# A one-core attention-and-MLP gradient kernel: the key feature gradient computed in its transposed layout

## The chip, the cores and the metric

The kernel runs on one core of a Trainium2 chip. The metric is the device time of one execution in microseconds (us). Three timed runs of the kernel before gave a median of 820.01 us.

## What is computed

One pre-norm layer is run forward and differentiated: 2048 rows (S) of 640 features (D), a linear-attention block with 32 heads of 20 features, and a gated MLP of width 1728 (F). The outputs are the layer's result and the gradients of the input, of `wqkv`, `wo`, `w1`, `w3` and `w2`. Cut to what matters:

```python
h  = x + A(layernorm(x));   h2 = h + B(layernorm(h))          # forward

def A(x, wqkv, wo):                       # linear attention
    q, k, v = split_heads(x @ wqkv)
    phi = lambda t: where(t > 0, t + 1, exp(t)) + 1e-6
    pq, pk = phi(q), phi(k)
    kv, z = pk^T v, sum_s(pk)             # per head
    o = (pq kv) / (pq . z + 1e-6)
    return o @ wo

def B(x, w1, w3, w2):                     # gated MLP
    return (silu(x @ w1) * (x @ w3)) @ w2

grads = vjp(h2 wrt x, wqkv, wo, w1, w3, w2)(grad_out)
```

The change is about the gradient of k, the input of `phi`. Since phi'(k) = min(pk, 1) up to the small constant, that gradient is `g_k = (xn @ gm + gz) * min(pk, 1)`, where `xn` is the normalised input, `gm` a 640x640 matrix (value weights times the gradient of `kv`) and `gz` the gradient of z, one number for each of the 640 features.

## The kernel before

The schedule is written by hand: every engine runs its instructions in the order of the code, and each DMA queue (SP's, ACT's and POOL's) does too. P = 128, the rows are 16 tiles of 128 (ST), the features five blocks of 128 (DT), W = 512 is a chunk of four row tiles, HD = 320. `dma` and `dmaT` are plain and transposing DMAs issued by SP, `dmaG` plain ones issued by POOL. The stages, with their times in the profile:

- 0 to about 84 us: layer norm, q and k, the key sums. `r_row(t)` makes row tile t of the normalised query features (`pqs[t]`), `r_T(t)` turns it into `pqT` by an SP transpose, `r_head` does both, and `r_store` writes it to DRAM (`r_d`) from POOL's queue.
- about 85 to 340 us: attention output, second layer norm (`f2_hn`, `f2_ht`), MLP forward. The row buffers of tag `pql` are four; `f2_hn(2)` takes the one that held `pqs[4]`.
- 340 to 535 us: gradients of w2 and of the MLP's input and attention's output. They end with `g_q` (the gradient of q, 16 row tiles) and `q_parts` (20 pieces of the gradient of kv), during which SP turns pieces into `QT` and loads turned weights and inputs (`load_xnT`, `load_wqT`).
- 560 to 611 us, called stage D here: small squares (`square`, `unload`), then the loop over 16 row tiles that makes `g_k`: ten matmuls of 320 columns with `xnT` as weights, a VectorE add of `gzb` (gz laid out as a row on all partitions, made by five matmuls with `ones`), and a VectorE op that takes min(pk, 1) and multiplies. `pk` comes in as eight row loads (`load_pk`). `fill(n)` puts n half jobs of the query weight gradient (eight matmuls of 320 columns each) between them; a job's result goes through `obs`, which has ten slots of 320 columns, and out by POOL's queue. Five squares for the value weight gradient are put in at t = 2, 5, 8, 11, 14; they too go out through `obs`, square n into slot pair k = 4, 0, 1, 2, 3.
- 611 to 698 us, stage E: `e_T(t, k)` turns row tile t of `g_q` and of `g_k` by SP transposes; `e_gxn(t)` multiplies 15 turned blocks (5 of q, 5 of k, 5 of `pkT`) with `wqT` and finishes the input's gradient (`ln_bwd`); jobs of the key weight gradient (`wq_jobs((1,))`) fill in before t = 0 and at every third t.
- 698 to 815 us, stage F: the w1 and w3 gradients, from `hnN` (rows of the second layer norm) and blocks `gb` that SP loads turned, 496 rows at a time, into two buffers.

PSUM tiles: `d_acc` takes two banks and has three buffers in stage D (tag `dkv`); it serves the g_k products, the squares and the small transposes in turn.

Of the kernel before, what the change touches and what calls it, by code (L numbers as in the profile page):

```python
# [9 lines left out]
P = 128  # L10
BF16 = mybir.dt.bfloat16
F32 = mybir.dt.float32
# [43 lines left out]
def kernel(  # L56
# [48 lines left out]
    def pool(name, side="left", space=None):  # L105
        kw = dict(space=space) if space is not None else dict(side=side)
        return tc.alloc_tile_pool(name=name, bufs=1, reuse_waits="tile", **kw)
# [195 lines left out]
    def phi_rest(keep=0):  # L303
        while len(held) > keep:
            held.pop(0)()
# [53 lines left out]
    def r_prod(t):  # L359
        for j in range(2):  # L360
            js = slice(j * HD, (j + 1) * HD)
            if t < 8:
                pr[t, j] = (p1.tile([P, HD], F32, name="pr", bufs=2) if t % 2 else
                            pf.tile([P, HD], F32, name="pr", tag="h2", bufs=2))[:]
            else:
                pr[t, j] = ps.tile([P, 512], F32, name="prp", tag="at", bufs=2)[:, 0:HD]
            (G if t < 8 else V).tensor_tensor(out=pr[t, j], in0=pqs[t][:, js], in1=Zb[:, js], op=ALU.mult)
# [16 lines left out]
    def r_T(t):  # L384
        dmaT(out=pqT[:, :, t * P:(t + 1) * P], in_=pqs[t])
# [47 lines left out]
    def m_end(m, js=(0, 1)):  # L433
        mb = mbs[:, m % 4, :]
        acc = macc[m]
        for j in js:
            A.copy(out=mb[:, j * HD:(j + 1) * HD], in_=acc[j][:, 0:HD])
        if m < 2:
            A.copy(out=Z[:, m:m + 1], in_=acc[1][:, HD:HD + 1])
            z_diag(m)  # L440
        if m < DT - 1:
            dmaT(out=mT[:, :, m * P:(m + 1) * P], in_=mb)
# [139 lines left out]
    def r_head(t):  # L582
        r_row(t)
        r_T(t)
# [24 lines left out]
    phi_rest()  # L609
    m_part(3, range(5))  # L610
    q_tile(6)
    r_head(1)
    r_prod(3)
    phi_rest()
    m_part(3, range(5, 11))
# [4 lines left out]
    phi_rest()  # L620
    m_part(3, range(11, ST))
    m_end(3)
    r_T(2)
    load_w2T(4 * P, 8 * P)
    dmaG(out=m_v[:, 1:4, :], in_=mbs[:, 1:4, :])
# [4 lines left out]
    kvT_block(1, big())  # L630
    r_row(4)
    r_prod(6)
    phi_rest()
    m_part(4, range(5, 11))
    q_tile(9)
# [308 lines left out]
    def kv3():  # L944
# [5 lines left out]
        (f2_wT, 4), (phi_rest,), (q_late, 14), (r_T, 4), (r_head, 5), (load_x, 4, 6), (r_prod, 7),  # L950
        (q_out, 10, 14), (mlp_ghh, 4),
        (q_late, 15), (w2_room,), (sig_table,), (f2_half, 0, 0), (f2_half, 1, 0), (f2_half, 2, 0), (f2_half, 3, 0), (mlp_ghh, 5),
        (f2_half, 0, 1), (r_store, 4, 5), (f2_half, 1, 1), (f2_hn, 0), (r_store, 5, 6), (f2_half, 2, 1), (f2_hn, 1),
        (f2_half, 3, 1), (f2_m_out,),
        (f2_half, 4, 0, True), (mlp_ghh, 6), (f2_half, 4, 1, True), (f2_half, 5, 0, True), (r_red, 6, (0,)), (f2_hn, 2), (f2_hn, 3),
        (f2_ht, 2), (f2_ht, 3), (load_w2T, 8 * P, 10 * P), (mlp_ghh, 7), (r_red, 6, (1,)), (r_inv, 6), (r_scale, 6),
        (r_T, 6), (f2_rest,), (r_red, 7), (r_inv, 7), (r_scale, 7), (r_T, 7), (r_store, 6, 7))
# [279 lines left out]
    def load_xnT(c):  # L1237

        if c % 2 == 0:
            both = ba.tile([P, 2, DT, W], BF16, name="xnT", tag="ggb", bufs=2)  # L1240
            xnT[c], xnT[c + 1] = both[:, 0], both[:, 1]
        dmaT(out=xnT[c], in_=xn_d[c * W:(c + 1) * W, :])
# [55 lines left out]
    def load_wqT(k):  # L1298
        dmaT(out=wqT[:, k * DT:(k + 1) * DT, :], in_=A_wqkv[:, k * D:(k + 1) * D])
# [11 lines left out]
    part(3)  # L1311
    load_xnT(1)
    part(4)
    part(4)
    part(20)
    load_xnT(2)
    V.reduce_sum(out=gz[:], in_=gz8[:], axis=AX.X)


# [72 lines left out]
        if i > 1:  # L1392
            fill(1)
    br.release()
    bo.release()
    bv = pool("bv")
    pkT = bv.tile([P, DT, S], BF16, name="pkT")
    small = bv.tile([P, ST, D], BF16, name="small", tag="hnN")
    mN, gkv_b, gm = (small[:, n:n + DT] for n in (0, DT, 2 * DT))
    gzd = small[:, 3 * DT, :].rearrange("p (m q) -> p m q", q=P)  # L1400
    dx = pool("dx", "right")

    def load_pk(c):
        pkb[c] = dx.tile([P, 2, D], BF16, name="pkb", bufs=4)
        (dma if c < 4 else dmaG)(out=pkb[c][:], in_=pk_v[:, c * 2:(c + 1) * 2, :])

    gzb = dx.tile([P, D], F32, name="gzb")
    g_k = gqkv[1] = U1.tile([P, ST, D], BF16, name="g_k", tag="S0")
    load_pk(0)
    load_pk(1)  # L1410
    dma(out=mN, in_=m_v)
    dma(out=rows(dwoT_d), in_=dwoT[:])
    load_pk(2)
    load_pk(3)
    load_xnT(3)
    load_wqT(0)

    for i, (c, ms) in enumerate(SQ_BLOCKS):
        unload(square(wqT[:, 2 * DT:, :], gkvT, i), gm[:, i, :])
        tr = ps.tile([P, len(ms), P], BF16, name="trk", tag="dkv", bufs=3)  # L1420
        for k, m in enumerate(ms):
            T.transpose(tr[:, k, :], gkvT[:, m, c * P:(c + 1) * P], ident[:])
        V.tensor_copy(out=gkv_b[:, c, ms[0] * P:(ms[-1] + 1) * P].rearrange("p (i q) -> p i q", q=P), in_=tr[:])
        fill(1)
        if i == 0:
            for m in range(DT):
                V.tensor_scalar(out=gzd[:, m, :], in0=ident[:], scalar1=gz[:, m:m + 1], scalar2=None, op0=ALU.mult)
        dmaT(out=wqT[:, 2 * DT:, i * P:(i + 1) * P], in_=gm[:, i, :])
    acc = d_acc()
    for m in range(DT):  # L1430
        T.matmul(acc[:, m // 4, m % 4 * P:(m % 4 + 1) * P], lhsT=ones[:], rhs=gzd[:, m, :], start=(m % 4 == 0),
                 stop=True, skip_group_check=True)
    for x, y, bank in ((0, 4 * P, 0), (4 * P, D, 1)):
        A.copy(out=gzb[:, x:y], in_=acc[:, bank, 0:y - x])

    for t in range(ST):
        c, i = divmod(t, TPC)
        u = t // 2
        acc = d_acc()
        for j in range(2):  # L1440
            for k in range(DT):
                T.matmul(acc[:, j, 0:HD], lhsT=xnT[c][:, k, i * P:(i + 1) * P], rhs=gm[:, k, j * HD:(j + 1) * HD],  # L1442
                         start=(k == 0), stop=(k == DT - 1))
        gp = dx.tile([P, D], F32, name="gp")
        V.tensor_tensor(out=two(gp[:]), in0=acc[:, :, 0:HD], in1=two(gzb[:]), op=ALU.add)
        V.scalar_tensor_tensor(out=g_k[:, t, :], in0=pkb[u][:, t % 2, :], scalar=1.0, in1=gp[:], op0=ALU.min,
                               op1=ALU.mult)
        if t % 2 and t < 13:
            fill(1)

        if t in (2, 5, 8, 11, 14):
            n = t // 3
            acc = square(mN, gkv_b, n)
            k = (4, 0, 1, 2, 3)[n]
            ob = obs[:, k * D:(k + 1) * D]
            unload(acc, ob)
            dmaG(out=out2S[:, n, 2 * D:3 * D], in_=ob)
        if t % 2 and u + 4 < 8:
            load_pk(u + 4)
        if t == 2:  # L1460
            load_wqT(1)
        if t in (6, 8, 10, 12):
            n = t // 2 - 3
            dmaT(out=pkT[:, :, n * W:(n + 1) * W], in_=pk_d[n * W:(n + 1) * W, :])
    for _ in jobs:
        pass
    dx.release()
# [1 line left out]


    ex = pool("ex", "right")
    hnN = bv.tile([P, ST, D], BF16, name="hnN")
    blocks = [(f0, min(f0 + NB, 2 * F)) for f0 in range(0, 2 * F, NB)]
    NB0 = 160

# [13 lines left out]
    def load_hnN(i):  # L1489
        dma(out=hnN[:, i * TPC:(i + 1) * TPC, :], in_=hn_v[:, i * TPC:(i + 1) * TPC, :])  # L1490

    gT = {}

    def e_T(t, k):
        if k == 0:
            gT[t] = (ex.tile([P, 2 * DT, P], BF16, name="gT") if t % 3 == 2 else
                     bd[:, 2 * (t % 3):2 * (t % 3) + 2, :].rearrange("p c (k q) -> p (c k) q", q=P))
        dmaT(out=gT[t][:, k * DT:(k + 1) * DT, :], in_=gqkv[k][:, t, :])

    def e_gxn(t):  # L1500
        acc = ps.tile([P, 2, 512], F32, name="gxn", tag="gxn", bufs=2)
        for j in range(2):
            for k in range(15):
                g = gT[t][:, k, :] if k < 2 * DT else pkT[:, k - 2 * DT, t * P:(t + 1) * P]
                T.matmul(acc[:, j, 0:HD], lhsT=g, rhs=wqT[:, k, j * HD:(j + 1) * HD], start=(k == 0),  # L1505
                         stop=(k == 14))
        gx = scr[:, t % 2, :]
        ln_bwd(acc, t, xnN[:, t, :], ln1, gx, g_h[:, t, :], ex, scr[:, 2 + t % 2, :], scr[:, 4, :])()
        return gx
# [3 lines left out]
    njob = 2  # L1513
    jobs = wq_jobs((1,))
    scr = U1.tile([P, DT, D], BF16, name="scr", tag="W6")
    for t in range(3):
        for k in range(2):
            fill(2)
            e_T(t, k)
    for t in range(ST):  # L1520
        if t > 1 and t % 3 == 0:
            fill(2)
        gx = e_gxn(t)
        if t + 3 < ST:
            for k in range(2):
                e_T(t + 3, k)
        dma(out=out1S[:, t, :], in_=gx)
        if t in (2, 3, 5, 6):
            load_hnN((2, 3, 5, 6).index(t))
        if t in (7, 9, 12):  # L1530
            load_block(0, (t - 7) // 2 * NB0, (t - 5) // 2 * NB0 if t < 12 else NB)
        if t == 13:
            load_block(1)
    for _ in jobs:
        pass

# [32 lines left out]
            gw2_turn(i)  # L1569
    ps.release()  # L1570
    ex.release()
    bv.release()
    bl.release()
    U1.release()
# [31 lines left out]
```

## Time and profile before

| | |
|---|---|
| median of three runs | 820.01 us (819.78 to 821.04) |
| profiled execution | 819.99 us |
| its span, first to last instruction | 817.9 us |
| TensorE matmul busy | 811.8 us, 5261 instructions |
| VectorE, ScalarE, GpSimd busy | 452.7, 324.8, 131.8 us |
| mean granted TensorE clock | 1.000 |
| DMA moved | 162.46 MB |

A view's line names the source line, the engine, the operation, what it writes and reads, and the shape. In a timeline the first number is the start in us from the span's start, the second the time to the end of the group, and "x10" the number of instructions that were merged. Matmuls are pipelined, so the spacing of starts, not the duration, says what one costs. About 2.1 us of the execution lie outside the span.

### The profile page before, as it was taken

To read this page: it belongs to the slowest core of one execution; us is meant where nothing else is said; L and a number is where in the kernel's file an instruction comes from. 1 tells how busy PE (TensorE), PEld (TensorE's weight loads), DVE (VectorE), ACT (ScalarE), POOL (GpSimd) and SP (SyncE) were. 2 spreads that over 40 slices of the span, in tenths; PEclk is the share of its full clock that TensorE was granted. 3 is DMA by queue.
4 is the path that set the end of the run, shared out by engine and by line. 5 is a ranking of instruction groups with operands and counts; after the bars stand their busy time and mean duration, and the time that the engine had idled before them with its cause. 6 is when DMAs were issued, how large, how long until landed. Compare 5 with 4: busy or idle time off the path is not lost.

```text
span 817.9 us, 13715 instructions
## 1 busy us (share of the span) xinstructions
PE 811.8 (99%) x5261; PEld 501.6 (61%) x5292; DVE 452.7 (55%) x973; ACT 324.8 (40%) x609; POOL 131.8 (16%) x198
## 2 busy tenths in 40 slices
PE   9999999999999999999999999999999999999998
PEld 6777544555555555754577777777777777544444
DVE  7859997998898566300057777772781544200000
ACT  7856688665565666011222212222212334211111
POOL 2243333333222212100001111110220000000000
PEclk9999999999999999999999999999999999999999
DMA  9799899696485556999967877266997888979991
GB/s 268 201 243 287 198 270 319 196 242 174 126 211 157 165 175 168 230 238 243 260 176 182 214 198 196 58 113 142 252 206 158 182 193 158 240 179 233 218 242 37
DMA packets 335761, 162.46 MB, mean 199 GB/s; under 512 B 252304, under 2 KB 328944, under 8 KB 335696
## 3 DMA queue, kind: packets, MB, share of 16 engines
q1 hardware_dynamic: 291936, 120.68, 63.9%
q0 software_dynamic: 7328, 24.48, 9.2%
q10 hardware_dynamic: 36432, 16.42, 8.0%
q8 instruction: 41, 0.67, 0.4%
q14 instruction: 24, 0.20, 0.1%
HBM read 47.09 MB, written 53.43 MB: 123 GB/s over the span
## 4 chain that ended last, share of the span: by engine, by line
PE 98%; ACT 1%; DVE 1%; issue 0%; POOL 0%; ACTq 0%
PE mm L395 20%; PE job L1335 20%; PE ghn L1131 14%; PE gxn L1505 8%; PE gw L1086 7%; PE big L268 4%; PE o L913 4%; PE o L859 3%; PE gwo L1219 3%; PE macc L430 3%; PE gr L1188 3%; PE dkv L1442 3%; PE at L657 2%; PE mm L268 1%; PE dkv L1369 1%; PE gp L395 1%
## 5 line engine op out<-in xcount | busy, mean ns | idle before, releaser
L1335 PE MATMUL job<-gb,hnN 128*128 128x496 bf16 (+3 forms) x576 | 116.8, 366 | 0.0
L1131 PEld LDWEIGHTS <-ggb 128*128 128x128 bf16 x864 | 84.5, 98 | 33.0
L395 PE MATMUL mm<-pqT,w 128*128 128x512 bf16 x396 | 93.2, 379 | 0.5
L1335 PEld LDWEIGHTS <-hnN 128*128 128x128 bf16 x576 | 55.7, 98 | 61.1
L395 PEld LDWEIGHTS <-w 128*128 128x128 bf16 x540 | 52.5, 98 | 63.2 <-issue 0.6
L1339 ACT CAST obs<-job 128x496 bf16<-128x496 f32 (+4 forms) x56 | 28.5, 509 | 123.7 <-PE job L1335 123.7
L1131 PE MATMUL ghn<-w13a,ggb 128*128 128x320 bf16 x448 | 63.5, 299 | 0.0
L1146 DVE SCALAR_TENSOR_TENSOR wb<-gs,hnb 128x640 f32<-128x640 bf16 x16 | 13.2, 825 | 88.1 <-ACT gs L1143 88.1
L1131 PE MATMUL ghn<-w13b,ggb 128*128 128x320 bf16 x416 | 61.4, 299 | 0.0
L395 PE MATMUL mm<-g2T,w2T 128*128 128x512 bf16 x228 | 58.9, 379 | 0.6
L1086 PE MATMUL gw<-hb,g 128*128 128x512 bf16 (+2 forms) x316 | 58.4, 345 | 0.2
L1086 PEld LDWEIGHTS <-g 128*128 128x128 bf16 x320 | 31.3, 98 | 27.0
L420 ACT CAST ghh<-mm 128x512 bf16<-128x512 f32 x48 | 28.1, 585 | 47.6 <-PE mm L395 41.2
L1196 POOL TENSOR_TENSOR sz<-Zb,g_h 128x640 f32<-128x640 bf16 x16 | 20.2, 1261 | 163.8 <-DVE g_h L1197 163.8
L796 ACT ACTIVATE sig<-mm 128x512 bf16<-128x512 f32 x56 | 33.7, 602 | 25.5 <-PE mm L395 21.7
L1143 ACT ACTIVATE gs<-ghn 128x640 bf16<-128x640 f32 x16 | 11.2, 703 | 75.9 <-PE ghn L1131 66.1
L395 PEld LDWEIGHTS <-w2T 128*128 128x128 bf16 x260 | 25.4, 98 | 23.4
L268 PEld LDWEIGHTS <-pqT 128*128 128x128 bf16 x320 | 30.8, 98 | 13.4 <-ACT pqT L260 1.3
L268 PE MATMUL big<-wqkv,pqT 128*128 128x320 bf16 x250 | 38.4, 299 | 0.3
L1335 PEld LDWEIGHTS <-g 128*128 128x128 bf16 x320 | 31.0, 98 | 11.6
L832 DVE TENSOR_TENSOR gate<-gate,sig 128x1024 bf16<-128x1024 bf16 x28 | 19.3, 690 | 33.8 <-ACT gate L807 31.0
L1091 ACT CAST gw2o<-gw 128x512 bf16<-128x512 f32 (+2 forms) x20 | 10.4, 519 | 66.7 <-PE gw L1086 25.6
(217 smaller groups left out, 1391.8 us busy)
## 6 DMA issues: line engine op xcount, KB each, us to landing
hh_d<-hhT SPq DMA_DIRECT2D x24, 256.0 KB, 2.7
gg_d<-gate POOLq DMA_DIRECT2D x24, 256.0 KB, 4.2
gg_d<-ghh POOLq DMA_DIRECT2D x24, 256.0 KB, 3.9
ggb<-gg_d SPq DMA_DIRECT2D x6, 896.0 KB, 5.3
ggb<-gg_d ACTq DMA_DIRECT2D x6, 832.0 KB, 5.4
ggb<-gg_d SPq DMA_DIRECT2D x2, 1728.0 KB, 12.6
x_sb<-in_A_x_dram SPq DMA_DIRECT2D x4, 640.0 KB, 4.7
pk_d<-pk_all SPq DMA_DIRECT2D x4, 640.0 KB, 5.3
```

The lines of the kernel that those rows point to most:

```text
L268: T.matmul(acc, lhsT=pqT[:, c, t * P:(t + 1) * P], rhs=wqkv[:, c, n0:n0 + HD], start=(c == 0), stop=(c == DT - 1))
L395: T.matmul(acc[:], lhsT=w[:, c, fc * P:(fc + 1) * P], rhs=rhs[:, c, :], start=(c == 0), stop=(c == DT - 1))
L420: A.copy(out=ghh[n // 2][:, n % 2, :], in_=acc[:])
L430: T.matmul(macc[m][j][:, 0:n], lhsT=pk_all[:, t, m * P:(m + 1) * P], rhs=x_ext[:, t, j * HD:j * HD + n], start=(t == 0), stop=(t == ST - 1))
L796: A.activation(sig[:, i, :], gp[:], AF.Sigmoid)
L859: T.matmul(accs[i, j][:, 0:HD], lhsT=hhT[c][:, fc, i * P:(i + 1) * P], rhs=w2[:, fc, j * HD:(j + 1) * HD], start=(first and fc == 0), stop ...
L913: T.matmul(o2["ps"][:, 0:HD], lhsT=hhT[c][:, fc, i * P:(i + 1) * P], rhs=w2[:, fc, j * HD:(j + 1) * HD], start=(fc == 0), stop=(fc == FT - 1))
L1086: T.matmul(acc[:, 0:fw], lhsT=g2[:, t, m * P:(m + 1) * P], rhs=hb[b][:, t, 0:fw], start=(t == 0), stop=(t == ST - 1))
L1131: T.matmul(acc[:, j, 0:HD], lhsT=ggb[t // 2][:, k, lo:lo + P], rhs=rhs[:, j * HD:(j + 1) * HD], start=(k == 0), stop=(k == NG - 1))
L1335: T.matmul(acc[:, 0:n], lhsT=lhs[:, t, m * P:(m + 1) * P], rhs=rhs(t), start=(t == 0), stop=(t == ST - 1))
L1339: A.copy(out=ob, in_=acc[:, 0:n])
L1505: T.matmul(acc[:, j, 0:HD], lhsT=g, rhs=wqT[:, k, j * HD:(j + 1) * HD], start=(k == 0), stop=(k == 14))
```

## The change

The gradient of k is now made transposed, `g_kT` (features on partitions, 2048 rows along the free axis), in 20 blocks n = (chunk c, feature block d): five matmuls of 512 columns with `gm` as weights and `xnT` as the moving operand. In this layout gz is one number for each partition, so it is a scalar operand and `gzb` is not made. min(pk, 1) is taken from `pkT`, the turned pk, which stage E read already; so `pkT` is loaded before and during stage D, and the eight row loads of pk are gone. Stage E reads `g_kT` as it stands and turns only `g_q`. The rows of `g_k`, which the key weight gradient needs, are made by 20 SP transposes out of `g_kT` (`k_turn`) during stage E, and all ten key weight jobs come after the last `e_gxn`. The five squares are now put in at n = 9, 11, 13, 15, 17, and the query weight jobs at every odd n below 16. `hnN` takes the memory of `g_q`, so its loads and those of the first `gb` blocks come later in stage E. In the early part, the transpose `r_T(1)` goes behind the one of `m_end(3)`, the store of r tile 4 goes out of its row step at once, and that of tile 5 goes behind `f2_m_out`.

```diff
     q_tile(6)
-    r_head(1)
+    r_row(1)
 ...
     m_end(3)
+    r_T(1)
     r_T(2)
 ...
     r_row(4)
     r_prod(6)
+    dmaG(out=r_v[:, 4, :], in_=pqs[4])
 ...
-        (f2_half, 0, 1), (r_store, 4, 5), (f2_half, 1, 1), (f2_hn, 0), (r_store, 5, 6), (f2_half, 2, 1), (f2_hn, 1),
-        (f2_half, 3, 1), (f2_m_out,),
+        (f2_half, 0, 1), (f2_half, 1, 1), (f2_hn, 0), (f2_half, 2, 1), (f2_hn, 1),
+        (f2_half, 3, 1), (f2_m_out,), (r_store, 5, 6),
 ...
     load_xnT(1)
     part(4)
+    load_wqT(0)
     part(4)
     part(20)
-    load_xnT(2)
+    bo.release()
+    bv = pool("bv")
+    pkT = bv.tile([P, DT, S], BF16, name="pkT")
+    def load_pkT(c):
+        dmaT(out=pkT[:, :, c * W:(c + 1) * W], in_=pk_d[c * W:(c + 1) * W, :])
+    load_pkT(0)
+    load_pkT(1)
 ...
-    load_pk(0)
-    load_pk(1)
-    dma(out=mN, in_=m_v)
     dma(out=rows(dwoT_d), in_=dwoT[:])
-    load_pk(2)
-    load_pk(3)
-    load_xnT(3)
-    load_wqT(0)
+    load_xnT(2)
 ...                                       # five small squares and SP transposes of gm into wqT, as before
-    acc = d_acc()
-    for m in range(DT):
-        T.matmul(acc[:, m // 4, m % 4 * P:(m % 4 + 1) * P], lhsT=ones[:], rhs=gzd[:, m, :], ...)
-    for t in range(ST):
-        acc = d_acc()
-        for j in range(2):
-            for k in range(DT):
-                T.matmul(acc[:, j, 0:HD], lhsT=xnT[c][:, k, i * P:(i + 1) * P], rhs=gm[:, k, j * HD:(j + 1) * HD], ...)
-        V.tensor_tensor(out=two(gp[:]), in0=acc[:, :, 0:HD], in1=two(gzb[:]), op=ALU.add)
-        V.scalar_tensor_tensor(out=g_k[:, t, :], in0=pkb[u][:, t % 2, :], scalar=1.0, in1=gp[:], op0=ALU.min, op1=ALU.mult)
-        if t % 2 and t < 13:
-            fill(1)
-        if t in (2, 5, 8, 11, 14):
-            acc = square(mN, gkv_b, n)
- ...
+    load_pkT(2)
+    dma(out=mN[:], in_=m_v)
+    load_xnT(3)
+    load_pkT(3)
+    load_wqT(1)
+    for n in range(SC * DT):
+        c, d = divmod(n, DT)
+        if d % 2 == 0:
+            acc = d_acc()
+        for k in range(DT):
+            T.matmul(acc[:, d % 2, :], lhsT=gm[:, k, d * P:(d + 1) * P], rhs=xnT[c][:, k, :], ...)
+        V.tensor_scalar(out=pm[:], in0=pkT[:, d, cs], scalar1=1.0, scalar2=None, op0=ALU.min)
+        V.scalar_tensor_tensor(out=g_kT[:, d, cs], in0=acc[:, d % 2, :], scalar=gz[:, d:d + 1], in1=pm[:], op0=ALU.add, op1=ALU.mult)
+        if n % 2 and n < 16:
+            fill(1)
+        if n > 8 and n % 2:
+            i = (n - 9) // 2
+            if i < DT:
+                sq = square(mN, gkv_b, i)
+                k = (4, 0, 1, 2, 3)[i]
+                ob = obs[:, k * D:(k + 1) * D]
+                unload(sq, ob)
+                dmaG(out=out2S[:, i, 2 * D:3 * D], in_=ob)
+    for t in range(DT):
+        e_T(t)
 ...
-    hnN = bv.tile([P, ST, D], BF16, name="hnN")
+    hnN = g_q
 ...
+    def k_turn(n):
+        c, d = divmod(n, DT)
+        dmaT(out=g_k[:, c * TPC:(c + 1) * TPC, d * P:(d + 1) * P], in_=g_kT[:, d, c * W:(c + 1) * W])
 ...
-    for t in range(3):
-        for k in range(2):
-            fill(2)
-            e_T(t, k)
     for t in range(ST):
-        if t > 1 and t % 3 == 0:
-            fill(2)
         gx = e_gxn(t)
-        if t + 3 < ST:
-            for k in range(2):
-                e_T(t + 3, k)
+        if t + DT < ST:
+            e_T(t + DT)
+        for n in (2 * t, 2 * t + 1):
+            if n < SC * DT:
+                k_turn(n)
         dma(out=out1S[:, t, :], in_=gx)
-        if t in (2, 3, 5, 6):
-            load_hnN((2, 3, 5, 6).index(t))
-        if t in (7, 9, 12):
-            load_block(0, (t - 7) // 2 * NB0, (t - 5) // 2 * NB0 if t < 12 else NB)
-        if t == 13:
-            load_block(1)
+        if t > 10 and t < 15:
+            load_hnN(t - 11)
+        if t in (11, 13, 15):
+            load_block(0, (t - 11) // 2 * NB0, (t - 9) // 2 * NB0 if t < 15 else NB)
+    load_block(1)
     for _ in jobs:
         pass
```

More of the change, by code (lines that the diff above doesn't have):

```diff
@@ L1394 @@
     br.release()
[L1395 to L1407, printed above, removed]
+    bs = pool("bs")
+    g_kT = bs.tile([P, DT, S], BF16, name="g_kT")
+    dx = pool("dx")
+    gm, gkv_b = (dx.tile([P, DT, D], BF16, name=n) for n in ("gm", "gkv_b"))
     g_k = gqkv[1] = U1.tile([P, ST, D], BF16, name="g_k", tag="S0")
-    load_pk(0)
-    load_pk(1)
-    dma(out=mN, in_=m_v)
     dma(out=rows(dwoT_d), in_=dwoT[:])
-    load_pk(2)
-    load_pk(3)
-    load_xnT(3)
-    load_wqT(0)
+    load_xnT(2)
     for i, (c, ms) in enumerate(SQ_BLOCKS):
@@ L1424 @@
         fill(1)
-        if i == 0:
-            for m in range(DT):
-                V.tensor_scalar(out=gzd[:, m, :], in0=ident[:], scalar1=gz[:, m:m + 1], scalar2=None, op0=ALU.mult)
         dmaT(out=wqT[:, 2 * DT:, i * P:(i + 1) * P], in_=gm[:, i, :])
-    acc = d_acc()
[L1430 to L1434, printed above, removed]
@@ L1436 @@
-    for t in range(ST):
-        c, i = divmod(t, TPC)
-        u = t // 2
-        acc = d_acc()
-        for j in range(2):
-            for k in range(DT):
-                T.matmul(acc[:, j, 0:HD], lhsT=xnT[c][:, k, i * P:(i + 1) * P], rhs=gm[:, k, j * HD:(j + 1) * HD],
-                         start=(k == 0), stop=(k == DT - 1))
-        gp = dx.tile([P, D], F32, name="gp")
-        V.tensor_tensor(out=two(gp[:]), in0=acc[:, :, 0:HD], in1=two(gzb[:]), op=ALU.add)
-        V.scalar_tensor_tensor(out=g_k[:, t, :], in0=pkb[u][:, t % 2, :], scalar=1.0, in1=gp[:], op0=ALU.min,
+    gT = {}
@@ new lines, in e_T @@
+    def e_T(t):
+        gT[t] = bd[:, t % DT, :].rearrange("p (k q) -> p k q", q=P)
+        dmaT(out=gT[t], in_=g_q[:, t, :])
+    mN = U1.tile([P, DT, D], BF16, name="mN", tag="W6")
+    load_pkT(2)
[5 more added lines that the diff above has]
+        c, d = divmod(n, DT)
+        cs = slice(c * W, (c + 1) * W)
+        if d % 2 == 0:
+            acc = d_acc()
+        for k in range(DT):
+            T.matmul(acc[:, d % 2, :], lhsT=gm[:, k, d * P:(d + 1) * P], rhs=xnT[c][:, k, :], start=(k == 0),
+                     stop=(k == DT - 1))
+        pm = dx.tile([P, W], BF16, name="pm", bufs=2)
+        V.tensor_scalar(out=pm[:], in0=pkT[:, d, cs], scalar1=1.0, scalar2=None, op0=ALU.min)
+        V.scalar_tensor_tensor(out=g_kT[:, d, cs], in0=acc[:, d % 2, :], scalar=gz[:, d:d + 1], in1=pm[:], op0=ALU.add,
@@ L1447 @@
                                op1=ALU.mult)
-        if t % 2 and t < 13:
+        if n % 2 and n < 16:
             fill(1)
-        if t in (2, 5, 8, 11, 14):
-            n = t // 3
-            acc = square(mN, gkv_b, n)
[L1454 to L1464, printed above, removed]
+        if n > 8 and n % 2:
[6 more added lines that the diff above has]
+                dmaG(out=out2S[:, i, 2 * D:3 * D], in_=ob)
@@ L1490, in load_hnN @@
         dma(out=hnN[:, i * TPC:(i + 1) * TPC, :], in_=hn_v[:, i * TPC:(i + 1) * TPC, :])
[L1492 to L1498, printed above, removed]
+    def k_turn(n):
+        c, d = divmod(n, DT)
+        dmaT(out=g_k[:, c * TPC:(c + 1) * TPC, d * P:(d + 1) * P], in_=g_kT[:, d, c * W:(c + 1) * W])
     def e_gxn(t):
@@ L1503, in e_gxn @@
             for k in range(15):
-                g = gT[t][:, k, :] if k < 2 * DT else pkT[:, k - 2 * DT, t * P:(t + 1) * P]
+                ts = slice(t * P, (t + 1) * P)
+                g = gT[t][:, k, :] if k < DT else g_kT[:, k - DT, ts] if k < 2 * DT else pkT[:, k - 2 * DT, ts]
                 T.matmul(acc[:, j, 0:HD], lhsT=g, rhs=wqT[:, k, j * HD:(j + 1) * HD], start=(k == 0),
@@ L1571 @@
     ex.release()
+    bs.release()
     bv.release()
```

## The prediction

> **What bounds the kernel now.** First the page, for the engine that is never idle and the chain that ended last.
>
> ```profile
> PE 811.8 (99%) x5261; PEld 501.6 (61%) x5292; DVE 452.7 (55%) x973; ACT 324.8 (40%) x609; POOL 131.8 (16%) x198
> PEclk9999999999999999999999999999999999999999
> PE 98%; ACT 1%; DVE 1%; issue 0%; POOL 0%; ACTq 0%
> ```
>
> TensorE is busy for 811.8 of 817.9 us at full clock and is 98% of the chain. So every edit has two prices only: TensorE instructions added or removed, and new holes in TensorE's stream. How many holes are there to close? The waits of TensorE, whole view:
>
> ```profile
> PE warm L468 <- DVE zero L125: 1.1, 1, 1.1
> PE trh L768 <- DVE hn L161: 0.3, 1, 0.3
> ```
>
> One is the start; the other, 0.3 us at `f2_ht`, is all that a reordering could win. Then the timeline of TensorE in stage D and at one MLP matmul: starts of neighbouring groups give the cost of each kind.
>
> ```profile
> 87.79 1.24 PE L395 MATMUL mm<-g2T,w2T 128*128 128x512 bf16 x5
> 88.87 0.30 PE L655 MATMUL at<-x_sb,ident 128*128 128x320 bf16 x1
> ...
> 579.14 0.44 PE L1431 MATMUL dkv<-small,ones 128*128 128x128 bf16 x5
> 579.42 2.88 PE L1442 MATMUL dkv<-small,xnT 128*128 128x320 bf16 x20
> 582.14 1.25 PE L1335 MATMUL job<-g_q,g 128*128 128x320 bf16 x8
> 583.22 1.52 PE L1442 MATMUL dkv<-small,xnT 128*128 128x320 bf16 x10
> 584.58 0.50 PE L1369 MATMUL dkv<-small 128*128 128x140 bf16 x6
> 584.91 0.30 PE L1442 MATMUL dkv<-small,xnT 128*128 128x320 bf16 x1
> ```
>
> A 512-column matmul costs 1.08/5 = 0.216 us, a 320-column one 1.36/10 = 0.136, a half job (eight) 1.08, a square 0.33.
>
> **TensorE's instructions.** g_k: 160 x 0.136 = 21.8 us becomes 100 x 0.216 = 21.6: -0.2. The five `ones` matmuls go: 579.42 - 579.14 = -0.28. Jobs, squares and the 480 `gxn` matmuls keep number and shape; they only change places. Together -0.5 us.
>
> **The early moves.** `hn` of tile 2 takes the buffer of `pqs[4]`, whose store POOL issues at 91.87 and whose landing takes up to 4.8 us (2.1/3.3/4.8 for the stores of L735).
>
> ```profile
> 94.52 0.48 DVE L374 TENSOR_REDUCE rden<-pr 128x16 f32<-128x320 f32 x1
> 95.31 0.80 DVE L161 TENSOR_SCALAR hn<-x_sb,ln_mv,ln_rs 128x640 bf16<-128x640 bf16 x2 [0.31 <-POOL ln_rs L155]
> ```
>
> VectorE's 0.31 us here is named after a POOL op, but 91.87 + 3.3 = 95.2 fits the store as well. After the change the store leaves at about 75 us and POOL carries no store between the `ln_rs` ops: the hole goes, -0.3 (0 if it was the POOL op of tile 3, which doesn't move; below nothing not more, as TensorE lost 0.3 there). `r_T(1)` behind the `mT` transpose swaps two SP entries of equal length (1.2 us); SP reaches the next ones when it did. Its readers come at 85 us, ten later. Nothing. Sum so far: -0.8.
>
> **Stage D's transfers.** SP's list from 562.7 us loses `load_xnT(2)`'s head start, four 0.45-0.7 us row loads and `load_wqT(0)` (3.7), gets two `pkT` loads ahead and two behind. The `wqT(0)` load now stands between turns of `QT`; SP is at it at 556.5, and with 3.7 us of issue the last turn still leaves near 562, as before; the products that need it start 565. In order: dwoT at 571.4, `xnT(2)`, five turns of gm (1.3 each, 576 to 582), then pkT(2), mN, `xnT(3)`, pkT(3) at 3.2 to 4 us each, `wqT(1)` until about 597, five `e_T` until 604. Needs on the same clock: mN at 595 (issued 585, landing some 5 later), chunk 2 at 596 (issued by 585), chunk 3 at 604 (issued by 593), `wqT(1)` and the first `g_q` turn at 611. Each has 5 us or more in hand, priced at nothing; without it, a rival below.
>
> **VectorE.** Each block is a min of 128x512 (0.32 us for the like op at 640 columns, so 0.26 to 0.32) and a two-operand op (0.825 at 640, so 0.66 at 512; 0.83 if the PSUM operand or fixed cost weighs). 0.96 a block against TensorE's 1.08 plus 0.54 of job in most: hidden.
>
> **A wait that the change adds.** Square 0 now writes slots 8 and 9 of `obs` at n = 9, and query job 8, whose result belongs in slot 8, ends at n = 11 (four half jobs ahead of the squares, three among them, five with gm, then n = 1, 3, ...: the 18th half is at n = 11). Before, the square was at t = 2 and that job at t = 11. So ScalarE's copy of job 8 must wait until square 0's store has landed. Behind it in ScalarE's order stands the unload of square 1, behind that VectorE's half of it, and behind that VectorE's work on n = 12 and 13, whose PSUM buffer n = 15 needs. Let X be the end of square 0 on TensorE. Before, a square's unload ran like this (ScalarE, VectorE, POOL for the square that ended at 591.50):
>
> ```profile
> 591.74 0.47 ACT L1375 CAST obs<-dkv 128x380 bf16<-128x380 f32 x1 [3.75 <-DMA out_dram<-obs]
> 592.31 0.42 DVE L1375 CAST obs<-dkv 128x260 bf16<-128x260 f32 x1
> 593.02 0.57 POOL L1457 DMA_DIRECT2D out_dram<-obs  x1 [3.46 <-DVE obs L1375]
> ```
>
> So the store is issued at X + 1.5 and lands at X + 1.5 + L. Then job copy 0.53, unload 0.52 and 0.52, two blocks of VectorE 2 x 0.96, hand-over 0.1: n = 15 may start at X + 5.1 + L. Unhindered it starts after n = 10 to 14 (5 x 1.08), two half jobs and two squares: X + 8.2. The hole is L - 3.1. What is L? The landing of these stores in stage D:
>
> ```profile
> out_dram<-obs POOLq DMA_DIRECT2D x5, 160.0 KB, 5.0
> DMA to landing us min/median/max: 3.3/5.0/6.8
> ```
>
> At 3.3 the hole is 0.2, at 5.0 it is 1.9, at 6.8 it is 3.7. I take L = 4.0: at X + 1.5 = 597 (579.1 + 16.6 + 1.5) the row loads of pk on POOL's queue (8.1 us median) are gone and SP has passed its long transposes, so the early-kernel stores (median 3.3) are as near as stage D's. Hole 0.9 us.
>
> The Trainium skill (DMA: Bandwidth & Descriptors, Queues, rings and completion order) says that each DMA engine takes turns between queues packet by packet, so a store from POOL would not stand behind SP's transposes; by that the hole would be nought and the time 819.2. The 5.0 us here against 3.3 us of equal-sized stores earlier speaks against it.
>
> **Stages E and F.** A tile of `gxn` is 30 x 0.136 = 4.1 us. SP per tile: one 128x640 turn 1.21, two `k_turn` (four 128x128 blocks instead of five, so an estimate of 1.0 each), a store 0.4: 3.6. A turn is issued four tiles (16 us) ahead of use and lands in 2.6. `g_k` is complete near 655, its jobs start at 676. `hnN` and block 0 are issued from 656 to 685, block 1 by 692; they are needed at 698 and 715. The tail of ten jobs (21.8 us) covers them; nothing. If that cover failed, the price is a landing of `gb`, 10 us median.
>
> **Sum.** 819.99 - 0.5 - 0.3 + 0.9 = 820.1; the profiled execution equals the median within 0.02.
>
> **Rivals.** *Store in time* (0.25): L at 3.3 or less, job 8 not held: 819.2 to 819.4.
>
> *SP late* (0.12, slower): if SP's list after 571 goes at the worst issue times of before (xnT 8.35 against 2.4 at best, `wqT` 6.9, 4.3 for a mean pkT), the sum is 0.4 + 8.4 + 6.5 + 4.3 + 0.4 + 8.4 + 4.3 + 6.9 = 39.6: `wqT(1)` leaves at 611 and lands at 613.5, the first turn at 615 against 611 needed: 3 to 4 us, 823. For it: DMA share over 1.0 from 572 to 612. Against: 2.6 MB of row loads are gone. It decides from SP passing `wqT(1)` at 607.
>
> *Long landing* (0.12): L from 5.4 on, hole 2.3 to 3.7: 821.5 to 822.9.
>
> *Clock* (0.01): throttling in stage D. Halving it there costs 100 x 0.216 = 21.6 us: 841.7. The clock row shows 9 in all slices, with 512-column streams over rotating PSUM buffers in the MLP too. The Trainium skill (TensorE: Matmul & The Clock Gate, A second HAM failure mode) warns of such an oscillation at 512 columns.
>
> **Chances.** Forecast 0.50 (L from 3.3 to 5.4: 819.4 to 821.5), store in time 0.25, long landing 0.12, SP late 0.12, clock 0.01. 0.2% of 820 is 1.64 us, about what a measurement can tell: faster needs 818.4, and -0.8 is all that I found to win, so 0.03, out of the store in time. Slower needs 821.65: SP late, most of the long landings, the clock: 0.22. The rest, 0.75. Range 819.0 to 822.2: the no-hole case below, most long landings above; SP late stays out.
>
> **What would show it.** Right: `ones` gone, 512-column matmuls 0.216 apart, no wait of `trh`; a ScalarE wait of job copy on the store `out_dram<-obs`, then a TensorE wait of about 1 us on `dkv` near 603. Wrong: TensorE waits on DMA in stages D or E, or a span shorter by over 1 us.

## The result and the profile after

| | before | after |
|---|---|---|
| median of five runs | 820.01 us (819.54 to 821.04) | 824.85 us (824.59 to 825.7) |
| span of the profiled execution | 817.9 us | 822.9 us |
| mean granted TensorE clock | 1.000 | 1.000 |

The ratio is 1.0057 [1.0046, 1.0069]: slower by 4.8 us. The prediction said 820.1, 819.0 to 822.2, so the time lies above its range and beyond what any of its rivals gave but the one on the clock, which did not move.

The page of the kernel after, its busy times and its chain:

```profile
PE 813.4 (99%) x5227; PEld 495.4 (60%) x5227; DVE 445.1 (54%) x976; ACT 324.9 (39%) x607; POOL 129.1 (16%) x194
PE 97%; DVE 1%; DMA 1%; ACT 1%; issue 0%; POOL 0%; DVEq 0%; ACTq 0%
```

Nothing alarming: TensorE still shows 99%. A share rounded to a percent of 820 us cannot show 5 us. TensorE's waits can (what waited, for what, us in total, times, longest):

```profile
PE dkv L1442 <- DVE g_kT L1446: 4.4, 5, 1.0
PE warm L468 <- DVE zero L125: 1.1, 1, 1.1
PE mm L395 <- DMA pqT<-hn: 0.5, 1, 0.5
```

The first line is new: five times a matmul of the new loop waits for VectorE's `g_kT` op. The timeline of TensorE shows where (start, time to the group's end, the wait in brackets):

```profile
579.33 1.24 PE L1442 MATMUL dkv<-xnT,gm 128*128 128x512 bf16 x5
581.42 1.24 PE L1442 MATMUL dkv<-xnT,gm 128*128 128x512 bf16 x5 [0.84 <-DVE g_kT L1446]
582.49 1.25 PE L1346 MATMUL job<-g_q,g 128*128 128x320 bf16 x8
583.58 1.24 PE L1442 MATMUL dkv<-xnT,gm 128*128 128x512 bf16 x5
585.66 1.24 PE L1442 MATMUL dkv<-xnT,gm 128*128 128x512 bf16 x5 [0.84 <-DVE g_kT L1446]
586.74 1.25 PE L1346 MATMUL job<-g_q,g 128*128 128x320 bf16 x8
587.83 2.32 PE L1442 MATMUL dkv<-xnT,gm 128*128 128x512 bf16 x10
589.99 1.25 PE L1346 MATMUL job<-g_q,g 128*128 128x320 bf16 x8
591.07 2.32 PE L1442 MATMUL dkv<-xnT,gm 128*128 128x512 bf16 x10
...
600.14 1.24 PE L1442 MATMUL dkv<-xnT,gm 128*128 128x512 bf16 x5 [1.00 <-DVE g_kT L1446]
...
604.92 1.24 PE L1442 MATMUL dkv<-xnT,gm 128*128 128x512 bf16 x5 [1.04 <-DVE g_kT L1446]
...
614.28 2.32 PE L1442 MATMUL dkv<-xnT,gm 128*128 128x512 bf16 x10 [0.64 <-DVE g_kT L1446]
616.44 0.84 PE L1497 MATMUL gxn<-wqT,bd 128*128 128x320 bf16 x5
```

Block n = 0 starts at 579.33 and takes 1.08; n = 1 starts at 581.42 and not at 580.41, 1.01 late. The waits stand at n = 1, 3, 11, 13 and 18, the second block of a pair that shares one PSUM tile (`acc` is taken at even d only), and only where no half job lies between the two: between n = 5 and n = 6 stands one (589.99), and n = 6 starts at 591.07 without a wait. By the spacing of starts the five cost 1.01 + 1.00 + 1.17 + 1.21 + 0.80 = 5.19 us. VectorE beside the first one:

```profile
579.38 0.28 DVE L1445 TENSOR_SCALAR pm<-pkT 128x512 bf16<-128x512 bf16 x1
580.61 0.75 DVE L1446 SCALAR_TENSOR_TENSOR g_kT<-dkv,gz,pm 128x512 bf16<-128x512 f32 x1 [0.95 <-PE dkv L1442]
```

VectorE itself waited 0.95 us for block 0. Its op starts 0.20 after TensorE could have gone on (the last matmul's results must be there), takes 0.75, and 0.06 after its end TensorE starts block 1: 0.20 + 0.75 + 0.06 = 1.01. Block 1 writes the other bank of the tile, yet its first matmul waits until VectorE has read the first one. The waits at n = 11 and 13 are longer by 0.2, because there VectorE comes to its op late, behind the unload of a square.

The span splits at 579 (start of the first `gm` or `ones` matmul) and at the end of the loop with its squares and eight half jobs, a set of work that is the same in both kernels. The loop after ends at 616.44, where the first `gxn` starts; the one before ends where the key weight jobs begin:

```profile
611.50 2.74 PE L1335 MATMUL job<-g_k,g 128*128 128x320 bf16 x19
```

| | before | after | difference |
|---|---|---|---|
| up to that loop | 579.14 | 579.33 | +0.19 |
| the loop | 32.36 (to 611.50) | 37.11 (to 616.44) | +4.75 |
| the rest | 206.4 | 206.5 | +0.1 |

So the whole loss lies in stage D, and 5.19 of waits less some 0.4 saved make it up.

### The profile page after: what moved, and what is told of

Same layout as the page of the kernel before. It is cut to its first block, busy times and chain, and to the rows that moved or that the text cites. A ratio compares the mean times of both kernels' runs of the same rounds, so it can differ in the third digit from the quotient of the medians.

```text
span 822.9 us, 13582 instructions
## 1 busy us (share of the span) xinstructions
PE 813.4 (99%) x5227; PEld 495.4 (60%) x5227; DVE 445.1 (54%) x976; ACT 324.9 (39%) x607; POOL 129.1 (16%) x194
## 4 chain that ended last, share of the span: by engine, by line
PE 97%; DVE 1%; DMA 1%; ACT 1%; issue 0%; POOL 0%; DVEq 0%; ACTq 0%
PE mm L395 20%; PE job L1346 19%; PE ghn L1133 14%; PE gxn L1497 8%; PE gw L1088 7%; PE big L268 4%; PE o L915 4%; PE o L861 3%; PE gwo L1221 3%; PE macc L430 3%; PE gr L1190 3%; PE at L659 3%; PE dkv L1442 2%; PE mm L268 1%; DVE g_kT L1446 1%; PE dkv L1380 1%
## 5 line engine op out<-in xcount | busy, mean ns | idle before, releaser
L1346 PE MATMUL job<-gb,g_q 128*128 128x496 bf16 (+3 forms) x576 | 116.8, 366 | 0.0
L1346 PEld LDWEIGHTS <-g_q 128*128 128x128 bf16 x576 | 55.8, 98 | 61.0
L1148 DVE SCALAR_TENSOR_TENSOR wb<-gs,hnb 128x640 f32<-128x640 bf16 x16 | 13.2, 825 | 88.1 <-ACT gs L1145 88.1
```

The source lines that it names most:

```text
L1346: T.matmul(acc[:, 0:n], lhsT=lhs[:, t, m * P:(m + 1) * P], rhs=rhs(t), start=(t == 0), stop=(t == ST - 1))
```

## The experiments

All times are us. "Loop" is the length of stage D's loop in the profiled execution, as in the table above. Experiments 1 to 4 ran on one chip, where the kernel before took 819.7, and 5 to 8 on it later, 819.98.

### e1_split_acc: a PSUM tile for each block

```diff
-        if d % 2 == 0:
-            acc = d_acc()
+        acc = d_acc()
 ...
-            T.matmul(acc[:, d % 2, :], ...
+            T.matmul(acc[:, 0, :], ...
```

> The changed kernel with a PSUM tile of its own for every block n of g_kT (first bank only), in place of one two-bank tile for two blocks. Theory (the second block of a pair waits for VectorE's read of the first because they share a tile): the five TensorE waits of 0.64 to 1.04 us on VectorE's g_kT op go, 4.5 to 5.2 us with the restart, so 819.7 to 820.4. Rival (VectorE is too slow for the loop, or the hardware holds TensorE while VectorE reads PSUM): the waits stay, only moved, 824 to 825.

Measured 821.32, ratio 1.0018 [1.0006, 1.0031]; loop 34.21: 0.9 above the forecast's range. The waits of the pairs are gone all the same. What is left in stage D, in TensorE's waits:

```profile
PE dkv L1380 <- DVE obs L1386: 1.4, 1, 1.4
PE dkv L1441 <- DVE g_kT L1445: 0.6, 1, 0.6
```

This is the other wait, the one that the prediction had worked out. ScalarE, VectorE and TensorE in the timeline, and in the fence behind it the store that they hang on (landing of the squares' stores, least, median, most):

```profile
602.76 0.42 ACT L1350 CAST obs<-job 128x320 bf16<-128x320 f32 x1 [6.39 <-DMA out_dram<-obs]
603.08 0.48 ACT L1386 CAST obs<-dkv 128x380 bf16<-128x380 f32 x1
...
603.60 0.43 DVE L1386 CAST obs<-dkv 128x260 bf16<-128x260 f32 x1 [4.66 <-ACT obs L1386]
...
604.08 0.49 PE L1380 MATMUL dkv<-gkv_b,mN 128*128 128x140 bf16 x6 [1.40 <-DVE obs L1386]
605.13 2.32 PE L1441 MATMUL dkv<-xnT,gm 128*128 128x512 bf16 x10 [0.56 <-DVE g_kT L1445]
```

```profile
DMA to landing us min/median/max: 2.1/2.1/5.5
```

Job 8's copy stands on ScalarE until square 0's store has landed; then come the square's unload on both engines and VectorE's blocks. By spacing TensorE loses 2.3 us: 1.57 before the square at 604.08, 0.72 before the block at 605.13. With 34.21 - 2.3 = 31.9 nothing else is lost in this loop.

### e2_job_between: a half job between the blocks of every pair

```diff
-        if n % 2 and n < 16:
+        if d in (0, 2):
             fill(1)
```

> The changed kernel with its eight half jobs after the blocks d = 0 and d = 2 of each chunk, so that 1.09 us of job stand between the two blocks of every pair; the tiles stay shared. Theory (shared tile): the wait of about 1 us is covered in all eight pairs, 819.7 to 820.4, as with tiles of their own. Rival (VectorE too slow): the work of both engines is the same, so 824 to 825. If the store of the first value-weight square held anything up, less of it shows here than with separate tiles, as the 18th half job comes one block later.

Measured 819.92, ratio 0.9998 [0.9989, 1.0006]; loop 32.13. The tiles are still shared and TensorE's list names no wait in stage D (x4 in the first line: a record is missing):

```profile
579.37 1.24 PE L1442 MATMUL dkv<-xnT,gm 128*128 128x512 bf16 x4
580.45 1.25 PE L1346 MATMUL job<-g_q,g 128*128 128x320 bf16 x8
581.54 2.32 PE L1442 MATMUL dkv<-xnT,gm 128*128 128x512 bf16 x10
```

The half job between n = 0 and n = 1 lasts 1.08, the wait 1.01. Job 8 now ends later, at n = 12, and its copy no longer meets the store of square 0 (it waits for TensorE). One line put elsewhere gives the 4.9 us back.

### e3_early_only: the kernel before with the early moves alone

```diff
-    r_head(1)
+    r_row(1)
 ...
+    r_T(1)
 ...
+    dmaG(out=r_v[:, 4, :], in_=pqs[4])
 ...                                    # and r_store(5) behind f2_m_out
```

> The kernel before with the early moves alone: r_T(1) behind the mT transpose, the stores of r tiles 4 and 5 moved. Theory (what is late next is the landing of the transpose of hn tile 1, which the moves do not bring forward): TensorE's wait at f2_ht goes and comes back 1.5 us later at the first MLP matmul, 819.9 to 820.3. Rival (the prediction's step): 819.7, 0.3 below the kernel before.

Measured 820.2, ratio 1.0001 [0.9992, 1.0009]: the interval runs from -0.7 to +0.7 us, so a gain of 0.3 is neither seen nor ruled out. The trace shows the mechanism of the forecast: `trh` does not wait, and the first MLP matmul starts at 99.39, 0.81 after TensorE could have gone on. The turned `hn` tile that it reads had just landed (issued at 96.07, landing 3.3 later). The list names ScalarE's `ghh` there (0.7), which ended at the same time.

### e4_no_min: without the min

The op that takes the min is left out and the second operand is `pkT` as it stands, so `g_k` and what follows from it are other numbers.

```diff
-        pm = dx.tile([P, W], BF16, name="pm", bufs=2)
-        V.tensor_scalar(out=pm[:], in0=pkT[:, d, cs], scalar1=1.0, ..., op0=ALU.min)
-        V.scalar_tensor_tensor(..., in1=pm[:], ...)
+        V.scalar_tensor_tensor(..., in1=pkT[:, d, cs], ...)
```

> The changed kernel without the op that takes min(pk, 1): the multiplication uses pkT itself, so g_kT is another number. Theory (shared tile): the min runs while TensorE works and is not in the wait, so the five waits keep their length, 824.3 to 825. Rival (VectorE too slow for the loop): 20 ops of 0.28 us less on VectorE, 5.6 us, and the waits shrink by a third or more, 820 to 823.

Measured 824.46, ratio 1.0053 [1.004, 1.0066]; loop 36.61.

```profile
PE dkv L1442 <- DVE g_kT L1444: 3.9, 5, 0.8
```

A quarter of VectorE's work in the loop is gone and all five waits are still there, shorter by 0.5 in all. What went are the parts of the waits at n = 11, 13 and 18 for which VectorE had come late behind a square's unload (1.00, 1.04 and 0.64 became 0.84, 0.84 and 0.51); the 0.84 at n = 1 and 3 stayed. VectorE is not short of time; TensorE waits for one particular op of it.

### e5_even: the half jobs after even n

```diff
-        if n % 2 and n < 16:
+        if n % 2 == 0 and n < 16:
             fill(1)
```

> The changed kernel with its eight half jobs after every even n below 16 in place of every odd n, nothing else. Theory (shared tile, wait wherever no other work stands between the two blocks of a pair): the pairs of even chunks (n = 0 and 1, 2 and 3, 10 and 11, 12 and 13) are now parted by a job and wait no more; those of odd chunks (5 and 6, 7 and 8) wait 1.0 us in full, the pairs 15 and 16 and 17 and 18, parted by a square of 0.33 us, some 0.7 each: 3.4 us in all, 822.5 to 824. Rival (something at those times, such as transfers, holds the loop): waits stay near 581, 585, 599 and 604 us, 824.5 to 825.

Measured 824.83, ratio 1.0055 [1.0042, 1.0068]; loop 36.35. The pairs of chunk 0 and the one at n = 10 are covered, and those of chunk 1, where d even means n odd, are laid bare, as are the two at the end:

```profile
581.56 2.32 PE L1442 MATMUL dkv<-xnT,gm 128*128 128x512 bf16 x10
...
590.14 1.24 PE L1442 MATMUL dkv<-xnT,gm 128*128 128x512 bf16 x5 [0.84 <-DVE g_kT L1446]
...
594.38 1.24 PE L1442 MATMUL dkv<-xnT,gm 128*128 128x512 bf16 x5 [0.84 <-DVE g_kT L1446]
...
604.78 1.24 PE L1442 MATMUL dkv<-xnT,gm 128*128 128x512 bf16 x5 [0.84 <-DVE g_kT L1446]
...
610.44 2.32 PE L1442 MATMUL dkv<-xnT,gm 128*128 128x512 bf16 x10 [0.51 <-DVE g_kT L1446]
...
613.60 2.32 PE L1442 MATMUL dkv<-xnT,gm 128*128 128x512 bf16 x10 [0.51 <-DVE g_kT L1446]
```

The waits move with the half jobs, to n = 6 and 8 (1.0 each), 16 and 18 (0.67 each), and those near 581, 585 and 599 are gone. The time missed the forecast all the same and lies in the rival's range, for two reasons. The one at 604.78 is n = 13, which has a half job ahead of it: there the store holds ScalarE again (its copy of a job at 602.41 waited on `out_dram<-obs`), the unload and n = 12 come late, and 1.0 is lost once more. And the loop, though 0.76 shorter than after, does not show in the median: the time outside the loop scatters as much, as told at the end of this section.

### e6_split_slots: own tiles, and square i in slot pair i

```diff
 ...                                    # e1_split_acc, and
-                k = (4, 0, 1, 2, 3)[i]
+                k = i
```

> Own tiles for every block (as in the run with separate tiles) and square i into slot pair i of obs, so that no query job's copy waits for a square's store. Theory (with the shared tile gone, job 8's copy waiting on square 0's store is what is left): ScalarE's 6.4 us wait on the store and TensorE's 1.4 and 0.6 us waits near 604 go; 2 us below the run with separate tiles, 819.0 to 819.8. Rival (those waits are VectorE's rate): no change, 821.

Measured 819.65, ratio 0.9992 [0.9981, 1.0002]; loop 31.94. TensorE's waits, all of them:

```profile
PE warm L468 <- DVE zero L125: 1.1, 1, 1.1
PE mm L395 <- DMA pqT<-hn: 0.8, 1, 0.8
PE k L268 <- DMA wqkv<-in_A_wqkv_dram: 0.3, 1, 0.3
```

The loop, from its first line to the one that ends it:

```profile
579.81 2.32 PE L1441 MATMUL dkv<-xnT,gm 128*128 128x512 bf16 x10
...
611.75 0.84 PE L1496 MATMUL gxn<-wqT,bd 128*128 128x320 bf16 x5
```

It is without a hole: 20 x 1.08 + 8 x 1.08 + 5 x 0.33 = 31.9. The 2.3 us that e1 had left were the slot's.

### e7_slots_only: square i in slot pair i, tiles shared

```diff
-                k = (4, 0, 1, 2, 3)[i]
+                k = i
```

> The changed kernel with square i in slot pair i of obs, tiles still shared. Theory (in the changed kernel the waits between the blocks give the store its time, so the held copy costs next to nothing): the waits of the pairs stay, 824 to 825. Rival (the held copy is part of what was lost): 822 to 823.5.

Measured 825.93, ratio 1.0067 [1.0052, 1.0081]; loop 37.20, as after (37.11), with the same five waits. The slot alone buys nothing while the pairs wait. The time is 0.9 above the forecast's range. The profiled execution came to the loop at 580.53, 1.2 later than after, and had lost all of that before the first MLP matmul (99.11 against 97.92); the intervals of the two kernels overlap, and no cause in the edit is seen.

### e8_between_slots: e2, square i in slot pair i, early part as before

```diff
-        if n % 2 and n < 16:
+        if d in (0, 2):
 ...
-                k = (4, 0, 1, 2, 3)[i]
+                k = i
 ...                                    # and the early moves undone
```

> The changed kernel with jobs after d = 0 and d = 2, square i in slot pair i, and the early part as in the kernel before. If all that the change lost is the pairs' wait, and the early moves give nothing, what is left is the 0.5 us of TensorE instructions saved: 819.0 to 819.8, at or just below the kernel before. If separate losses remain in the transfers of stages D and E, 820 or more.

Measured 819.44, ratio 0.9996 [0.9987, 1.0004]; loop 32.17. Not to be told from e2 or from the kernel before.

What the loop leaves of the span, 785.5 before and 785.8 after, was 785.6 to 787.2 in these eight (the loop started at 579.1 to 580.8): that scatter of over 1 us is why loops that differ by 0.2 to 0.8 gave medians that cannot be ordered. The traces show where it arises. From the first MLP matmul (97.72 to 99.39) to the loop it is 481.4 us in nine of the ten profiles and 481.9 in e4. From the end of the loop to the end of the span it is 206.4 to 206.5 in all ten, so stages E and F cost the same in every kernel. The scatter lies in the first 98 us, where TensorE's waits differ from run to run: for the load of `wqkv` up to 0.9, for a turned `x_sb` 1.1 in e3 and 0.3 in e7. Of the three mended versions e6 has the shortest loop, 0.42 under before; none is shown to beat the kernel before.

## Why the prediction was wrong

**VectorE "hidden": the step that failed.** The prediction set 0.96 us of VectorE a block against 1.08 of TensorE "plus 0.54 of job in most", a comparison of rates. The rate came out a little higher, 1.05 (one op of VectorE starts at 608.85, the next block's at 609.90), still below TensorE's, and e4 shows that it did not matter. What it left out is a dependence: two blocks of a pair lie in one PSUM tile, and the second may not begin before the first has been read. The prediction even used the pair, for the rotation of buffers ("whose PSUM buffer n = 15 needs"), but did not ask who reads the tile between its two writes. The price was in the rows: VectorE's op, 0.66 to 0.83 by its own estimate, and the hand-over, in each pair with no job between. The half jobs stand after odd n, so these are the pairs at n = 0, 2, 10 and 12, and the one at 17, which has only a square (0.33). Five times about 1 us, 5.19 in all, were left out of the sum, where 0.9 of another wait was put in. e1, e2 and e6 take the wait away in two ways, by tile and by order, and the loop falls by 5.0 (e2) and 5.2 (e6, with the slot moved too).

The pause is one of the program's order, not of the memory: in e6 TensorE writes one bank while VectorE reads another all through the loop of 31.94 and no time is lost. The Trainium skill (PSUM — Partial Sum Buffer, The four PSUM rules) says that each bank is a separate memory; the trace agrees.

**TensorE's instructions.** Predicted -0.48. The `ones` are gone, the 512-column matmuls stand 0.216 apart (1.08 / 5), and e6's loop is 0.42 shorter than before's. Right.

**The early moves.** Predicted -0.3; no gain can be seen. The wait of `trh` did go, as the step said: `hn` of tile 2 starts at 94.86 (before 95.31) and `trh` at 95.41 (before 95.81). But the next thing is late at once:

```profile
95.41 0.94 PE L770 MATMUL trh<-ident,hn 128*128 128x128 bf16 x10
...
96.18 1.24 PE L395 MATMUL mm<-g2T,w2T 128*128 128x512 bf16 x5
...
97.92 2.33 PE L395 MATMUL mm<-pqT,w 128*128 128x512 bf16 x10 [0.49 <-DMA pqT<-hn]
```

The first MLP matmul needs a turned `hn` tile, whose transpose lands when it did (97.7 before, 97.9 after); the matmul started at 97.72 before. The prediction asked where a stall goes at stage D, but not here. Over all profiles that matmul starts at 97.72 to 99.39 in the eight with the moves and at 97.72 and 98.58 in the two without, and e3's median cannot tell 0.3 us.

**The added wait.** The chain was right in its form: the copy of job 8 behind the store, the unload behind the copy, VectorE behind the unload. In e1, where no pair hides it, the store was issued 1.42 after square 0's end (predicted 1.5), landed 5.5 later, and by "the hole is L - 3.1" TensorE should lose 2.4; it lost 2.3. That nearness is in part luck: in e1 every block takes a buffer of its own, so the hole fell before square 2 and n = 14, and not at n = 15. In the changed kernel L was 3.05, and the waits at n = 11 had already put job 8's end off, so that the copy found the store landed (602.38 against the copy at 602.54). So the 0.9 of the sum was not paid, and the size stays a matter of L: 3.05, 3.9 in e2, 5.5 in e1. The rivals *store in time* and *long landing* thus both had their condition met in some kernel, and neither had the price that counted. One reason given for L = 4.0 failed: SP had not passed its long transposes when the store left at 599.33, `wqT(1)` was out from 595.82 to 602.67. In that kernel POOL's `obs` stores issued from 572 to 602 us took 2.8 to 6.7 to land, those issued later 1.9 to 2.7; whether SP's loads are the cause is not shown. As to the turns that a DMA engine takes between queues (the Trainium skill, DMA: Bandwidth & Descriptors, Queues, rings and completion order): landings of 2.1 and 5.5 in one kernel do not settle it, and no run here took the other queue's transfers away.

**Transfers of stages D and E.** Priced at nothing, and in the changed kernel no TensorE wait on a DMA is seen after 98 us. The last load of `wqT` landed at 602.67 and the first `g_q` turn at 603.19, against 616.44 needed. A `k_turn` took 1.26 of SP (median) and not the estimated 1.0, so SP ran later than thought, and still block 1 landed at 701.45, in time. *SP late* falls: SP passed `wqT(1)` at 600.0, not after 607. The order is not without risk, though: in e4 a turn of `QT`, issued at 562.22 behind the `wqT(0)` load that the change put there, landed 4.2 later, and TensorE lost 0.5 at 566.49.

**Clock.** 1.000 in every run; the oscillation of which the Trainium skill warns (TensorE: Matmul & The Clock Gate, A second HAM failure mode) is not seen with 512 columns over three rotating buffers.

**What stays open.** Why the same store landed in 3.05 in one kernel and 5.5 in another, and why the waits of the first 98 us scatter by over 1 us.

## What to carry to other kernels

When two results share a PSUM tile, ask whether anything reads the tile between their writes: if so, the second's first matmul pays the drain, the reader's whole duration and the hand-over (here 0.20 + 0.75 + 0.06), however idle the reader's engine is. Either give each its own tile or put independent matmuls of at least that length between the two, and see where an index such as "after odd n" falls against the pairs. A gain from a removed stall counts only after looking at what lands next, and a busy share of 99% hides a 5 us loss that the list of waits shows in one line.

## What the runs showed of the hardware

VectorE's two-operand op on 128x512 with one f32 operand in PSUM took 0.751 us, against 0.825 for the like op on 128x640 with bf16 operands (L1148): 1.47 ns a column against 1.29, so the estimate scaled by columns (0.66) was 0.09 short. Two shapes cannot tell whether the PSUM operand or a fixed cost of an op makes the difference.

```profile
L1446 DVE SCALAR_TENSOR_TENSOR g_kT<-dkv,gz,pm x20: 749/751/752, 580.6 to 616.6; 128x512 bf16<-128x512 f32 x20
```
